# Sparse attention, dense FFN and soft MoE on one core: two transposes, four load places and one exponential moved

## The chip, the cores and the metric

The program runs on one core of one Trainium2 chip. The metric is the time of one execution on the device in microseconds (us). Several executions are timed and their median is given. One further execution is profiled, and all rows below come from that one. PE is the matrix engine, PEld its weight loads, DVE the vector engine, ACT the scalar engine, POOL GpSimd, SP the engine whose queue issues every DMA of this kernel.

## The reference

Three stages follow each other over 2304 tokens of 512 features, all in float32. The change lies in the third.

```python
x = attention(q, k, v)                 # 4 batches, 8 heads, 576 positions, local and strided masks
h = x @ w_in                           # 512 -> 2048
x = (h * sigmoid(1.702 * h)) @ w_out   # 2048 -> 512
logits = x @ phi                       # 512 -> 32 slots (8 experts of 4 slots)
d = exp(logits - logits.max(0)); d /= d.sum(0) + 1e-9       # softmax over the tokens
slot_input = d.T @ x                                        # 32 x 512
for e in range(8):                                          # experts, 512 -> 1024 -> 512
    slot_out[e] = relu(slot_input[e] @ w1[e]) @ w2[e]
c = exp(logits - logits.max(1)); c /= c.sum(1) + 1e-9       # softmax over the slots
out = c @ slot_out
```

## The kernel before

The tokens are worked through in five chunks, four of 512 and a last one of 256 (`CHUNKS`, numbers 0 to 4). For each chunk PE makes 16 blocks of `h` (line 489), ACT and DVE turn each into a gated block `gT` (lines 494 and 499), and DVE transposes it (line 527). The second matrix is never applied to the tokens: PE adds up logits from a product of `w_out` and `phi` (line 519), and `weighted` (line 626) adds up `u`, the gated blocks weighted by the slot softmax. Since the softmax over tokens needs the maximum of all tokens, each chunk lowers a running maximum (`nmx`), and the sums so far are scaled by `al`.

`combine_weights` makes the softmax over the slots of a chunk into `ca`. To be used on PE at the end, `ca` has to be split into a rounded part and the rest (`combine_split`, lines 639 and 640, tiles `c4`) and transposed on PE (`combine_t`, line 644, tiles `ctp`), and ACT copies the result to SBUF (`cT`, line 645).

`post_last` is the end of the last chunk. In order it does this: the last four logit products (line 656); the transposes of the combine weights of chunks 0 and 1; the logits repeated over the partitions (`lr`, line 667) and transposed (`lp`, line 674); the last maximum (DVE, lines 670 and 671); the exponential `l4` with its sum `zp` (ACT, line 679); its transposition `dT` (DVE, line 682); the sum `z` and its inverse, folded into `selz` (DVE, lines 684 to 690); `u` from `dT` (PE, line 626); the combine weights of chunk 4 (DVE and ACT, lines 710 to 718); and the copies of `u` out of PSUM (line 701). PE, DVE and ACT follow the written order here; POOL and SP don't. Then come `ut` (lines 699 and 882), its transposition (line 883), `spp` with `w_out` (line 890), `si`, the first expert products `hp` (`expand1`, line 922), the hidden transposes `hT` (line 933), the second expert products `op` (`expand2`, line 952) in three column groups of 256, 128 and 128, and after each group the final products `fp` (`combine`, line 968), whose copies leave by DMA (line 974). In the first column group, before the change, `expand2` number 5, 6 and 7 are each followed by the split and the transposes of one more chunk of combine weights (2, 3 and 4).

`load_ex` issues 36 loads of 1 MB: 0 to 3 are `w_out` (written earlier to DRAM), 4 to 19 the first expert matrices, 20 to 35 the second. Each load goes to the next free place: six in the pool `e1p` (tag `e`, loads 0 to 5), places of `x` tiles (tags `xA0`, `xA1`, `xB0`, `xB1`, `xC0`, `xC1`), places of `w_in` (tag `wi`) and quarters of `gT`. A load is issued when the last reader of its place is done, and the SP queue issues in order, so one load that waits holds up those behind it. Two tiles that are no loads also take `e` places: `hz`, the zero-padded hidden layer that POOL clears (line 980), and `hc`, the hidden layer before its transposition. A third, `fin`, holds the slot outputs.

Of the kernel before, what the change touches and what calls it, by code (L numbers as in the profile page):

```python
# [10 lines left out]
F32 = mybir.dt.float32  # L11
F32R = mybir.dt.float32r
# [5 lines left out]
AF = mybir.ActivationFunctionType  # L18
ALU = mybir.AluOpType
# [6 lines left out]
NS = NE * SPE  # L26
# [10 lines left out]
NF = FF // 128  # L37
# [43 lines left out]
def tile_kernel(ctx: ExitStack, tc: tile.TileContext, lqk, lv, sqk, sv, wraw, phi, wexp, cst, cstb, out):  # L81
    nc = tc.nc
# [53 lines left out]
    ca = keep.tile([P, NT // 128, NS], F32, name="ca")  # L136
    wp = keep.tile([P, NF, NS], F32, name="wp")
    
# [491 lines left out]

    def combine_split(c, parts):
        c0, N = CHUNKS[c]
        n = N // 128 // len(parts)
        c4s[c] = [t[:, 128 * k:128 * k + 128] for t in parts for k in range(n)]
        for k, t in enumerate(parts):
            c4 = t[:, :128 * n].rearrange("p (u r e q) -> p u r e q", r=2, e=2, q=8)
            ce = ca[:, c0 // 128 + n * k:c0 // 128 + n * k + n]
            cc = ce.rearrange("p t (j q) -> p (t j) q", q=8).unsqueeze(2).to_broadcast([P, 4 * n, 2, 8])
            nc.vector.tensor_copy(c4[:, :, :, 0].bitcast(F32R), cc)
            nc.vector.tensor_tensor(c4[:, :, :, 1].bitcast(F32R), cc, c4[:, :, :, 0], op=ALU.subtract)  # L640

# [5 lines left out]
    def post_last():  # L647
# [7 lines left out]
        def lg(j):  # L655
            nc.tensor.matmul(lgs[c][32 * j:32 * j + 32, :N], wp[:, NF - 4 + j, :], gs[c, NF - 4 + j][:, :N], start=False, stop=True)

        for j in range(3):
            lg(j)
# [17 lines left out]
        st["L"] = L  # L677
        zp = keep.tile([P, 1], F32, tag="zp", name=f"zp_{c}", bufs=2)
        nc.scalar.activation(l4[:, :N], lr[:, :N], AF.Exp, bias=nmx, accum_out=zp)
        al = keep.tile([P, 1], F32, tag="al", name=f"al_{c}", bufs=2)  # L680
        nc.scalar.activation(al, st["nm"], AF.Exp, scale=-1.0, bias=nmx)
        nc.vector.transpose(dT[:, :N], l4[:, :N])
        z = keep.tile([P, 1], F32, tag="z", name=f"z_{c}", bufs=2)
        nc.vector.scalar_tensor_tensor(z, st["z"], al, zp, op0=ALU.mult, op1=ALU.add)  # L684
        zi = keep.tile([P, 1], F32, name="zi")
# [179 lines left out]
    for s in side:  # L865
        for _ in s:
            pass
    load_ex(xp, "xB0")
    c = len(CHUNKS) - 1
    man = ctx.enter_context(ExitStack())  # L870
    man.enter_context(tc.manual_schedule(engines={mybir.EngineType.PE, mybir.EngineType.DVE, mybir.EngineType.Activation}))
    while todo:
        g_transpose(*todo.pop(0))
    ut, ub, halves, selz = post_last()
    for _ in range(2):
        load_ex(None, gx_tile())
# [20 lines left out]
    for h in range(2):  # L897
# [4 lines left out]
        st["si"] = (nc.vector.tensor_copy if h else nc.scalar.copy)(si[:, 2 * h:2 * h + 2], sip[:, :64].rearrange("p (k s) -> p k s", s=NS)).ins  # L902
    c4t = tl.tile([P, 2, 512], F32, name="c4t")
    cTs[3] = tl.tile([P, 512], F32R, name="cT3")
    moe_ps.close()
    ps_t = ctx.enter_context(tc.tile_pool(name="ps_t", bufs=3, space=PSUM))

    def ttile(name):
        return ps_t.tile([P, 512], F32, tag="t", name=name)

    hzt = e1p.tile([P, 2, 8, P], F32, tag="e", name="hz")
    hc = e1p.tile([P, 4, 512], F32, tag="e", name="hc")
    load_ex(e1p, "e")
    load_ex(xp, "xB1")
# [74 lines left out]
    expand1(1, 0)  # L989
    for _ in range(4):  # L990
        load_ex(wip, "wi")
    hidden_t(0, 1)
    expand1(1, 1)
    for _ in range(2):
        load_ex(wip, "wi")
    assert len(ex) == 36
# [3 lines left out]
    for n in range(8):  # L1000
        expand2(0, n)
        if n == 2:
            hidden_t(1, 1)
        if n >= 5:
            with tc.issue_after(st["si"]):
                combine_split(n - 3, [c4t[:, n % 2]])
            combine_t(n - 3, ttile(f"ctp_{n - 3}"))
    slot_out(0)
# [81 lines left out]
```

## Time and profile before

| | |
|---|---|
| median of 3 runs | 394.07 us (393.07 to 394.52) |
| profiled execution, its own time | 394.75 us |
| span of the profiled execution | 393.0 us |
| PE busy | 372.6 us, 95% of the span |
| DVE, ACT, POOL busy | 275.0, 214.5, 52.1 us |
| DMA | 91.25 MB, mean 232 GB/s |

The span runs from the first to the last instruction of the profiled execution; its own time lies 1.75 us above it. Busy shares are means over stages with different limits, so what the change touches has to be read from its own stretch, from 327 us to the end. PEclk in a row is the granted clock of PE as a share of the full 2.4 GHz: 0.50 is the lower of its two levels, 1.2 GHz.

### The profile page before, as it was taken

How to read it: one execution, taken by the hardware profiler on the slowest of the kernel's cores; microseconds unless marked ns; L12 is line 12 of the kernel's file. 1: busy time of each engine (PE TensorE's matmuls, PEld its weight loads, DVE VectorE, ACT ScalarE, POOL GpSimd, SP SyncE). 2: the span in 40 equal slices, each digit the busy share in tenths (PEclk: the TensorE clock that was granted, in tenths of full speed). 3: DMA queues.
4: the chain of work that ended last, by engine and by line, in shares of the span. 5: the costliest groups of instructions: out<-in, count | busy, mean ns of one | idle time of the engine just before them, and what ended most of it. 6: DMA issues, size and time to landing. Idle time of an engine off the chain costs nothing.

```text
span 393.0 us, 9638 instructions
## 1 busy us (share of the span) xinstructions
PE 372.6 (95%) x3874; PEld 261.2 (66%) x3875; DVE 275.0 (70%) x595; ACT 214.5 (55%) x585; POOL 52.1 (13%) x64
## 2 busy tenths in 40 slices
PE   8969999999999999999999899999999998899992
PEld 4757888877667574767476657767877786234682
DVE  3989899999788668988896888674446855321232
ACT  5977999899795745568446686302113123200331
POOL 1533346331020101001100010000000000100000
PEclk9988999999999999999999999999999999899997
DMA  8975294668753160497526646991008899879997
GB/s 300 416 293 200 81 327 143 228 211 311 262 199 111 53 207 9 129 319 267 203 86 196 200 150 214 315 398 78 0 2 318 332 330 362 304 282 419 420 373 237
DMA packets 29372, 91.25 MB, mean 232 GB/s; under 512 B 2448, under 2 KB 10768, under 8 KB 25232
## 3 DMA queue, kind: packets, MB, share of 16 engines
q1 hardware_dynamic: 29328, 90.64, 64.5%
q8 instruction: 30, 0.49, 0.5%
q14 instruction: 14, 0.11, 0.1%
HBM read 80.93 MB, written 8.91 MB: 229 GB/s over the span
## 4 chain that ended last, share of the span: by engine, by line
PE 64%; DVE 19%; ACT 10%; issue 2%; DMA 2%; POOL 0%; SPq 0%; ACTq 0%; DVEq 0%
PE h L489 38%; PE op L952 4%; ACT ts L273 4%; PE hp L922 4%; DVE gT L527 3%; PE av L333 2%; PE lg L519 2%; PE ptp L299 2%; PE u L626 2%; DMA raw<-wraw 2%; PE fp L968 2%; DVE nmx L260 2%; ACT neg L393 1%; PE s L219 1%; DVE acc L614 1%
## 5 line engine op out<-in xcount | busy, mean ns | idle before, releaser
L489 PE MATMUL h<-x,wi 128*128 128x512 f32 (+1 forms) x960 | 215.4, 377 | 0.5 <-DVE more L499 0.4
L489 PEld LDWEIGHTS h<-x,wi 128*128 128x128 f32 x960 | 165.4, 190 | 48.0 <-issue 14.6
L494 ACT ACTIVATE gT<-h 128x512 f32<-128x512 f32 (+1 forms) x50 | 27.0, 540 | 45.5 <-PE h L489 45.3
L284 POOL TENSOR_TENSOR ts<-ts,sm 128x384 f32<-128x384 f32 (+2 forms) x32 | 27.6, 862 | 140.0 <-DVE sm L280 112.5
L499 DVE SCALAR_TENSOR_TENSOR gT<-gT,h 128x512 f32<-128x512 f32 (+1 forms) x50 | 30.5, 612 | 21.2 <-ACT gT L494 20.9
L273 ACT ACTIVATE ts<-ts,nmx 128x96 f32<-128x96 f32 (+1 forms) x98 | 34.2, 352 | 9.1 <-DVE nmx L260 9.1
L393 ACT ACTIVATE neg<-raw,ebias 128x512 f32<-128x512 int16 x48 | 36.4, 759 | 0.0
L527 DVE STREAM_TRANSPOSE gT<-gT 128x512 f32<-128x512 f32 (+1 forms) x50 | 31.4, 633 | 2.0 <-PE lg L519 1.1
L428 POOL TENSOR_TENSOR wi<-wc,wi 128x512 fp32r<-128x512 f32 x16 | 21.7, 1369 | 31.8 <-ACT wi L424 31.8
L626 PE MATMUL u<-gT,dT 32*32 32x512 f32 x576 | 23.1, 633 | 2.4 <-DVE z L684 1.6
L494 ACT ACTIVATE more<-h 128x512 f32<-128x512 f32 (+1 forms) x19 | 10.6, 558 | 26.4 <-PE h L489 26.4
L299 PE MATMUL ptp<-cs,ts 128*96 128x128 f32 (+1 forms) x120 | 17.3, 278 | 6.0 <-POOL ts L284 3.4
L299 PEld LDWEIGHTS ptp<-cs,ts 128*96 128x96 f32 (+1 forms) x120 | 13.1, 132 | 11.2 <-POOL ts L284 6.0
L366 DVE TENSOR_TENSOR x<-av,x 128x320 fp32r<-128x320 f32 (+18 forms) x48 | 17.8, 403 | 1.2 <-ACT x L362 1.0
L362 ACT CAST x<-av 128x320 fp32r<-128x320 f32 (+18 forms) x48 | 16.2, 407 | 4.5 <-PE av L333 2.1
L273 ACT ACTIVATION_READ_ACCUMULATOR ts<-ts,nmx 128x1 f32 x98 | 18.6, 190 | 0.0
L626 PEld LDWEIGHTS u<-gT,dT 32*32 32x32 f32 x576 | 9.7, 104 | 12.4 <-issue 8.8
L519 PE MATMUL lg<-gT,wp 128*32 128x512 f32 (+1 forms) x92 | 17.7, 562 | 0.0
L333 PEld LDWEIGHTS av<-pt,v 96*64 96x64 f32 (+2 forms) x552 | 13.9, 136 | 4.6 <-issue 2.0
L499 DVE SCALAR_TENSOR_TENSOR more<-more,h 128x512 f32<-128x512 f32 (+1 forms) x19 | 12.0, 634 | 6.8 <-ACT more L494 6.4
L980 POOL MEMSET hz<- 128x512 f32 x4 | 1.9, 526 | 107.7 <-PE spp L890 107.7
L219 PE MATMUL s<-qk 64*64 64x96 f32 (+1 forms) x552 | 15.7, 236 | 0.3 <-DMA qk<-lqk 0.3
(173 smaller groups left out, 501.5 us busy)
## 6 DMA issues: line engine op xcount, KB each, us to landing
ex<-wexp SPq DMA_DIRECT2D x28, 1024.0 KB, 7.6
raw<-wraw SPq DMA_DIRECT2D x48, 511.8 KB, 4.4
v<-lv SPq DMA_DIRECT2D x8, 576.0 KB, 6.3
qk<-lqk SPq DMA_DIRECT2D x7, 608.0 KB, 6.8
wo_scr<-wo SPq DMA_DIRECT2D x16, 256.0 KB, 2.3
ex<-wo_scr SPq DMA_DIRECT2D x4, 1024.0 KB, 11.5
gT<-wexp SPq DMA_DIRECT2D x4, 1024.0 KB, 5.9
qk<-sqk SPq DMA_DIRECT2D x6, 604.0 KB, 5.7
```

Source lines behind the costliest of these rows:

```text
L273: nc.scalar.activation(ts[:, u], src[:, u], AF.Exp, scale=sc, bias=nmx[:, u:u + 1], accum_out=sm[:, u:u + 1])
L284: nc.gpsimd.tensor_tensor(ts, ts, sm[:, :nt].unsqueeze(2).to_broadcast([P, nt, nk]), op=ALU.mult)
L299: nc.tensor.transpose(ptp[:nk, u], src, ident)
L333: nc.tensor.matmul(avs[b, hp, e][64 * h:64 * h + 64, o:o + nq], v[k0:k0 + nk, P * w + 64 * h:P * w + 64 * h + 64], pt[k0:k0 + nk, p, 64 * ...
L393: nc.scalar.activation(n, top, AF.Relu, scale=-(2.0 ** 19), bias=ebias)
L428: nc.gpsimd.tensor_tensor(w[:, 1], conv.pop((f, 0)), w[:, 0].bitcast(F32), op=ALU.subtract)
L489: nc.tensor.matmul(h[:, :N], w[:, we, 128 * kt:128 * kt + 128], x[xe][:, kt, :N], start=kt + n == 0, stop=kt == 3 and n == 2)
L494: st["tanh"] = nc.scalar.activation(g[:, :N], hs[c, f][:, :N], AF.Tanh, scale=0.851).ins
L499: st["gate"] = nc.vector.scalar_tensor_tensor(g[:, :N], g[:, :N], 1.0, hs.pop((c, f))[:, :N], op0=ALU.add, op1=ALU.mult).ins
L519: nc.tensor.matmul(lgs[c][32 * j:32 * j + 32, :N], wp[:, f0 + j, :], gs[c, f0 + j][:, :N], start=f0 == 0, stop=f0 == NF - 4)
L527: nc.vector.transpose(t_slots(c)[:, f, :N], gs[c, f][:, :N])
L626: nc.tensor.matmul(us[a][32 * j:32 * j + 32, :].rearrange("p (t f) -> p t f", f=32), dT[q, 32 * b:32 * b + 32], gT[q, :, 32 * b:32 * b + 3 ...
```

## The change

The change has three parts.

First, the combine weights of chunks 2 and 3 are split and transposed in `post_last`. The split is done by POOL and ACT instead of DVE, into a new tile `c4x` at the place `xB0`, which the last chunk's `x` leaves free when the last product of `h` is done. The eight transposes stand on PE behind `lp`. ACT copies them behind `al`, chunk 3 to the place of `wp`. Because `c4x` now lies at `xB0`, load 21, which went there, is issued after `post_last`. The split and transposes of chunk 4 stay near the end, on DVE and PE.

Second, the last exponential is made in two halves of 128 columns, each with its own sum and its own transposition, and one addition joins the sums.

Third, two loads are asked for ahead of `hz` and `hc`, and two behind them, where it was one behind them. In the built program loads 24 to 27 now get the places of loads 0 to 3, `hz` that of load 5, `hc` that of load 4, and `fin` later that of `hc`. Before, load 24 got that of load 0, `hc` that of load 1, `hz` that of load 2, `fin` that of load 3. The loads behind move up by three places: the last, 35, takes the place of load 15 where it took that of load 18.

```diff
-    wp = keep.tile([P, NF, NS], F32, name="wp")
+    wp = keep.tile([P, NF, NS], F32, tag="wp", name="wp")
...
-    def combine_split(c, parts):
+    def combine_split(c, parts, high=nc.vector, low=nc.vector):
...
-            nc.vector.tensor_copy(c4[:, :, :, 0].bitcast(F32R), cc)
-            nc.vector.tensor_tensor(c4[:, :, :, 1].bitcast(F32R), cc, c4[:, :, :, 0], op=ALU.subtract)
+            (high.copy if high is nc.scalar else high.tensor_copy)(c4[:, :, :, 0].bitcast(F32R), cc)
+            low.tensor_tensor(c4[:, :, :, 1].bitcast(F32R), cc, c4[:, :, :, 0], op=ALU.subtract)
...
+        cx = xp.tile([P, 2, 512], F32, tag="xB0", name="c4x")
+        combine_split(3, [cx[:, 1]], nc.gpsimd, nc.gpsimd)
+        combine_split(2, [cx[:, 0]], nc.scalar, nc.gpsimd)
         for j in range(3):
             lg(j)
...
-        zp = keep.tile([P, 1], F32, tag="zp", name=f"zp_{c}", bufs=2)
-        nc.scalar.activation(l4[:, :N], lr[:, :N], AF.Exp, bias=nmx, accum_out=zp)
+        cTs[3] = keep.tile([P, 512], F32R, tag="wp", name="cT3")
+        ctps = [htile(f"ctp_{k}") for k in (2, 3)]
+        for k in (2, 3):
+            for n, t in enumerate(c4s[k]):
+                nc.tensor.transpose(ctps[k - 2][:, 128 * n:128 * n + 128], t, ident)
+        zp = keep.tile([P, 2], F32, name=f"zp_{c}")
+        for n in range(2):
+            t = slice(128 * n, 128 * n + 128)
+            nc.scalar.activation(l4[:, t], lr[:, t], AF.Exp, bias=nmx, accum_out=zp[:, n:n + 1])
+            nc.vector.transpose(dT[:, t], l4[:, t])
         al = keep.tile([P, 1], F32, tag="al", name=f"al_{c}", bufs=2)
         nc.scalar.activation(al, st["nm"], AF.Exp, scale=-1.0, bias=nmx)
-        nc.vector.transpose(dT[:, :N], l4[:, :N])
+        for k in (2, 3):
+            nc.scalar.copy(cTs[k], ctps[k - 2])
         z = keep.tile([P, 1], F32, tag="z", name=f"z_{c}", bufs=2)
-        nc.vector.scalar_tensor_tensor(z, st["z"], al, zp, op0=ALU.mult, op1=ALU.add)
+        nc.vector.scalar_tensor_tensor(z, st["z"], al, zp[:, 0:1], op0=ALU.mult, op1=ALU.add)
+        nc.vector.tensor_tensor(z, z, zp[:, 1:2], op=ALU.add)
...
-    load_ex(xp, "xB0")
...
     ut, ub, halves, selz = post_last()
+    load_ex(xp, "xB0")
...
+    for _ in range(2):
+        load_ex(e1p, "e")
     hzt = e1p.tile([P, 2, 8, P], F32, tag="e", name="hz")
     hc = e1p.tile([P, 4, 512], F32, tag="e", name="hc")
-    load_ex(e1p, "e")
+    for _ in range(2):
+        load_ex(e1p, "e")
     load_ex(xp, "xB1")
...
-        if n >= 5:
+        if n == 5:
             with tc.issue_after(st["si"]):
-                combine_split(n - 3, [c4t[:, n % 2]])
-            combine_t(n - 3, ttile(f"ctp_{n - 3}"))
+                combine_split(4, [c4t])
+        if n == 7:
+            combine_t(4, ttile("ctp_4"))
```

On PE, around the last maximum, the order was this (`lr` and `lp` are the two forms of the last logits, `ctp_3990` the transposes of chunk 1).

```order
-L665 MATMUL ctp_3990<-cs,gT 128x128 x4
-L667 MATMUL lr_3995<-l_4_3914,rep_r 128x256
-L674 MATMUL lp_4001<-rep_r,l_4_3914 128x32 x2
-L626 MATMUL u_0_4019<-gT,dT_3915 32x512 x4
-L626 MATMUL u_1_4020<-gT,dT_3915 32x512 x4
```

It is now this (`ctp_4010` and `ctp_4011` are the transposes of chunks 2 and 3).

```order
+L668 MATMUL ctp_3993<-cs,gT 128x128 x4
+L670 MATMUL lr_3998<-l_4_3914,rep_r 128x256
+L677 MATMUL lp_4004<-rep_r,l_4_3914 128x32 x2
+L685 MATMUL ctp_4010<-cs,c4x 128x128 x4
+L685 MATMUL ctp_4011<-cs,c4x 128x128 x4
+L626 MATMUL u_0_4038<-gT,dT_3915 32x512 x4
```

Eight transposes stand between `lp` and the first of `u`.

On PE, in the first column group of the second expert products, the order was this.

```order
-L952 MATMUL op_4265<-ex_4138,hz 32x256 x8
-L644 MATMUL ctp_4325<-cs,c4t 128x128 x4
-L952 MATMUL op_4265<-ex_4163,hz 32x256 x8
-L644 MATMUL ctp_4341<-cs,c4t 128x128 x4
-L952 MATMUL op_4265<-ex_4165,hz 32x256 x8
-L644 MATMUL ctp_4357<-cs,c4t 128x128 x2
```

It is now this (the same five products `op` from the fourth on).

```order
+L967 MATMUL op_4285<-gT,hz 32x256 x8
+L967 MATMUL op_4285<-ex_4154,hz 32x256 x8
+L967 MATMUL op_4285<-ex_4156,hz 32x256 x8
+L967 MATMUL op_4285<-ex_4160,hz 32x256 x8
+L967 MATMUL op_4285<-ex_4162,hz 32x256 x8
```

No transposes are left there; the two of chunk 4 moved ahead of the first hidden transposes.

On DVE, behind the last maximum, the order was this.

```order
-L671 TENSOR_TENSOR nmx_3998<-nmx_3998,nmx_3613 128x1
-L682 STREAM_TRANSPOSE dT_3915<-l_4_3914 128x256
-L684 SCALAR_TENSOR_TENSOR z_4011<-z_3623,al_4008,zp_4006 128x1
-L686 TENSOR_SCALAR zi<-z_4011 128x1
-L687 RECIPROCAL zi<-zi 128x1
```

It is now this.

```order
+L674 TENSOR_TENSOR nmx_4001<-nmx_4001,nmx_3613 128x1
+L690 STREAM_TRANSPOSE dT_3915<-l_4_3914 128x128 x2
+L696 SCALAR_TENSOR_TENSOR z_4029<-z_3623,al_4025,zp_4020 128x1
+L697 TENSOR_TENSOR z_4029<-z_4029,zp_4020 128x1
+L699 TENSOR_SCALAR zi<-z_4029 128x1
```

The transposition became two, and one addition stands ahead of the inverse; the rest of the DVE row, down to the copies of `u`, kept its order.

## Rows read from the trace of the kernel before

**Rows 1.** Chain that ended last, from 331 us on: start us, us, what.

```profile
332.75 3.53 PE u L626 x64
...
337.52 0.56 PE ut L882 x8
...
338.11 0.46 DVE dT L883
...
366.31 0.59 PE ctp L644 x4
...
386.10 0.37 ACT gT L971
```

**Rows 2.** Timeline, 327.8 to 333.2: start us, us, engine, line, operation [idle before].

```profile
327.93 0.38 ACT L494 ACTIVATE gT<-h 128x256 f32<-128x256 f32 x1 [1.05 <-PE h L489]
...
330.64 0.53 PE L674 MATMUL lp<-rep_r,l 128*128 128x32 f32 x4
...
331.56 0.47 ACT L679 ACTIVATE l<-lr,nmx 128x256 f32<-128x256 f32 x1
...
332.16 0.45 DVE L682 STREAM_TRANSPOSE dT<-l 128x256 f32<-128x256 f32 x1 [0.69 <-ACT l L679]
332.53 0.18 DVE L684 SCALAR_TENSOR_TENSOR z<-z,al,zp 128x1 f32<-128x1 f32 x1
```

**Rows 3.** PE alone in two stretches: busy (instructions), granted clock, DMA share, GB/s.

```profile
329.93:333.34 3.41, 1.83 (x41) 1.00 0.98 375
333.34:336.76 3.42, 3.42 (x71) 0.50 0.55 232
```

**Rows 4.** The products of line 626 alone, chunk 3: PE, PEld, clock, DMA.

```profile
303.00:308.00 5.00, 4.45 (x128) 2.20 (x128) 1.00 0.86 346
```

**Rows 5.** PE alone in two early stretches, columns as in rows 3.

```profile
15.90:19.32 3.42, 2.94 (x36) 1.00 1.03 419
19.32:22.73 3.41, 2.37 (x63) 1.00 1.04 415
```

**Rows 6.** Of these the transposes of line 299 alone: PE, PEld, clock, DMA.

```profile
15.90:19.32 3.42, 2.34 (x18) 1.84 (x18) 1.00 1.03 419
```

**Rows 7.** Timeline of DVE, 334.9 to 337.3.

```profile
335.00 0.22 DVE L718 TENSOR_TENSOR ca<-ca,cz 128x64 f32<-128x64 f32 x1
336.12 1.08 DVE L701 COPY gT<-u 128x256 f32<-128x256 f32 x3 [0.89 <-PE u L626]
```

**Rows 8.** POOL's instructions by line: shortest/median/longest in ns, first and last start.

```profile
L284 POOL TENSOR_TENSOR ts<-ts,sm x32: 720/830/1271, 12.5 to 233.6; 128x384 f32<-128x384 f32 x16, 128x480 f32<-128x480 f32 x8, 128x320 f32<-128x320 f32 x8
...
L428 POOL TENSOR_TENSOR wi<-wc,wi x16: 1265/1296/1759, 8.3 to 80.9; 128x512 fp32r<-128x512 f32 x16
```

**Rows 9.** DMA by stretch: length, granted clock, DMA share, GB/s.

```profile
334.00:350.00 16.00, 0.91 0.71 263
350.00:384.00 34.00, 1.00 1.02 405
...
386.00:390.00 4.00, 0.74 1.02 300
```

**Rows 10.** Last load, issued within 358.8 to 359.0: KB, us to landing.

```profile
ex<-wexp SPq DMA_DIRECT2D x1, 1024.0 KB, 20.2
```

**Rows 11.** Fifth output from the end: issue, and KB and us to landing.

```profile
385.23 0.77 SPq L974 DMA_DIRECT2D out<-gT  x1
...
out<-gT SPq DMA_DIRECT2D x1, 256.0 KB, 4.2
```

**Rows 12.** Last output: issue, and KB and us to landing.

```profile
388.83 0.82 SPq L974 DMA_DIRECT2D out<-gT  x1
...
out<-gT SPq DMA_DIRECT2D x1, 128.0 KB, 3.2
```

**Rows 13.** Small transfers elsewhere in the kernel, median us to landing.

```profile
wo_scr<-wo SPq DMA_DIRECT2D x16, 256.0 KB, 2.3
```

**Rows 14.** Timeline of PE, 381.7 to 383: the last second expert products.

```profile
381.78 1.08 PE L952 MATMUL op<-ex,hz 128*32 128x128 f32 x32
```

More of the change, by code (lines that the diff above doesn't have):

```diff
@@ L902, in tile_kernel @@
         st["si"] = (nc.vector.tensor_copy if h else nc.scalar.copy)(si[:, 2 * h:2 * h + 2], sip[:, :64].rearrange("p (k s) -> p k s", s=NS)).ins
-    c4t = tl.tile([P, 2, 512], F32, name="c4t")
-    cTs[3] = tl.tile([P, 512], F32R, name="cT3")
+    c4t = tl.tile([P, 256], F32, name="c4t")
     moe_ps.close()
@@ L989, in tile_kernel @@
     expand1(1, 0)
-    for _ in range(4):
-        load_ex(wip, "wi")
+    load_ex(wip, "wi")
     hidden_t(0, 1)
     expand1(1, 1)
-    for _ in range(2):
-        load_ex(wip, "wi")
     assert len(ex) == 36
```

## The prediction

> **What bounds the kernel now.** I read the page first. PE is busy 95% of the span, so a stretch counts only where PE waits or runs slowly, or where the end waits for something else. Then I read the chain that ended last, from 331 us on [rows 1]. It has two parts. Up to 338.11 it goes through the end of the last softmax: maximum, exponential, transposition, `u`, and the transposition of `ut`. From there it is PE nearly without a gap to the last products `fp`, and the last copy ends at 386.10 + 0.37 = 386.47.
>
> In the timeline [rows 2] the reader should see PE's only long gap here: `lp` ends at 331.17, `u` begins at 332.75 [rows 1]. PE has nothing to do in the 1.58 us in which ACT makes the exponential and DVE transposes it. The windows on PE [rows 3] show the price of that gap. PE is busy 1.83 of 3.41 us from 329.93 on, and from 333.34 to 336.76 its granted clock is 0.50, the lower level. `u` falls into it: 64 products in 3.53 us [rows 1], 0.055 us each, where chunk 3 did 128 in 4.45 us at the full clock [rows 4], 0.035 each. At that rate 64 take 2.23 us, so the fallen clock costs `u` alone 1.30 us.
>
> The DMA windows [rows 9] show a second bound. From 334 to 350 the transfers are busy 0.71 of the time, so 16 x 0.29 = 4.6 us lie idle while loads wait for places. From 350 to 384 they are at 1.02 without a break, and in 386 to 390 again, when only outputs are left. The fifth output from the end lands 4.2 us after its issue [rows 11], the last one 3.2 us [rows 12], at 388.83 + 3.2 = 392.0; elsewhere in the kernel as small a transfer lands in 2.3 us [rows 13]. So the outputs queue behind something, and part of the last 5 us is DMA, not PE.
>
> **Part 1a, transposes beside the last maximum.** Eight transposes move. In the tail each group of four takes 0.59 us on the chain [rows 1], and there are two such groups: 2 x 0.59 = 1.18 us leave PE's path. In their new place they run from 331.17 to 332.35, inside the gap, if their input is ready. The input comes from POOL: one copy and two subtractions of 128x256 each, after the last product of `h`, that is from about 327.93, when ACT's activation of it begins [rows 2]. POOL shows no copy and no such form. The nearest rows are 128x320 to 128x480 at 0.72 to 1.27 us and 128x512 at up to 1.76 us [rows 8]. Three at the shortest, 0.72, give 2.2 us and readiness at 330.1; three at the longest, 1.76, give 5.3 us and 333.2. By size these are smaller than any of them, so I take 2.2 us: 1 us ahead of need. If that cover went, each us beyond 3.2 would push `u` by one. ACT's own copy of chunk 2 stands behind the activation at 327.93 and ahead of the copy of chunk 0's transposes, for which ACT waits anyway; its two copies to `cT` follow `al`, in the time in which DVE is at `z` and its inverse and asks nothing of ACT. I cost them at nothing; if that cover were gone they would hold up line 713 and with it line 718.
>
> **Part 1b, the clock.** With the transposes PE is busy nearly without a gap to the start of `u`, so I expect the clock to stay at 1.00 and `u` to take 2.23 us. Does transposing hold the clock? From 15.90 to 19.32 PE is busy 2.94 us [rows 5], 2.34 of them transposes [rows 6], and the clock stays at 1.00 in that stretch and the next. By this row it holds. The Trainium skill ("TensorE: Matmul & The Clock Gate", Part 4: PE-mode transpose) says otherwise, that the full clock does not engage for transposes because they don't count as PE work in the same way. By that rule the clock would fall here as before; the early stretch speaks against it. The rule is priced as a rival below.
>
> **Part 2, the halved exponential.** The whole one runs from 331.56, and its transposition starts 0.60 us later and takes 0.45 [rows 2]. A half has 128 columns less; from these rows I estimate its transposition to start near 332.0 and take 0.3, so that `u` starts near 332.4, 0.3 us sooner. The second half ends near 332.3, its transposition near 332.6, and `u` needs it 1.1 us after its start. But DVE's row goes on: `z` at 332.53 [rows 2] stays about there, and the added joining of the sums puts 0.2 us (0.18 for line 684, [rows 2]) ahead of everything up to line 718.
>
> **What is late next.** With `u` ending at 332.4 + 2.23 = 334.65, its copies no longer wait for PE but for DVE, which finishes line 718 at 335.22 now [rows 7] and 335.42 then. Two copies of 0.36 (1.08 for three, [rows 7]) end at 336.14, the last products of `ut` need about 0.5 more (0.56 for eight, [rows 1]), so the transposition at line 883 starts near 336.7 instead of 338.11 [rows 1]: 1.4 us sooner. The 0.3 us of the halved exponential is thereby hidden; it counts only where the clock stays low. Bounds: 0.3 us if it does, 1.5 if the half works out a little better.
>
> **Part 3, the loads.** Loads 24 to 27 are issued as `spp` reads loads 0 to 3, where one of them could go before. Load 21 moves back from the last product of `h` to about 332.4, gated by the transposes, and holds up the two `gT` loads behind it not at all, since these wait for `u`. The idle 4.6 us of DMA are largely filled. PE gains nothing by it: the last load now lands at 358.9 + 20.2 = 379.1 [rows 10] and its product starts after 381.78 [rows 14]. That cover of 2.7 us would be used up by the 2.6 us that PE gains, so without the earlier loads the gain would be at its limit; with them it has room. `hz` waits for load 5 and `hc` for load 4, both read early in the first expert products, well before DVE writes into `hz`. The outputs gain: the loads end sooner by up to the 4.6 us filled and by what PE gains, so that outputs don't queue behind them. The last five hold 1.15 MB, 3.9 us at 300 GB/s [rows 9]. Their first issue moves from 385.23 to 382.6; landing after 2.3 [rows 13] instead of 4.2 us and then one per 0.88, the last lands near 388.1, instead of 392.0. That is 3.9 in all, 1.3 beyond PE's 2.6. The lower bound is zero, if the queue stays as long. I take 0.8.
>
> **The sum.** 1.4 + 1.18 + 0.8 = 3.4 us. Against the profiled execution, 394.75, that gives 391.35. The median is 0.7 below it and the fastest run, 393.07, 1.7 below, about what a fall of the clock costs, so some executions may not have it. For such a one only 1.18 + 0.8 less 0.2 for the addition is to gain: 393.07 - 1.8 = 391.3. Both meet, and I say **391.3**.
>
> **Rivals.** *The clock falls anyway*, by the transposes not holding it or by the short gaps that now lie near 335.6 and 336.8. For it: in rows 3 a busy time of 1.83 of 3.41 was followed by the low level, and the new gaps lie close together. Against it: rows 5 and 6. Then 0.3 + 1.18 + 0.8 = 2.3 remain: 392.5. The page's rule gives just this case. Chance 0.16. *The loads are not what holds the outputs*, as their landing is simply slow: 1.4 + 1.18 = 2.6, so 392.1. For it: DMA is also full in 386 to 390 with outputs alone. Chance 0.11. *POOL is late*, the slower side: at 5.3 us `u` starts at 333.2 + 1.2 = 334.4, 1.7 later than now, the clock falls as before, 1.18 is won in the tail, and 0.5 is lost: 395.2. It turns to a loss where the three take over 4.8 us. Against it: every POOL row of less than 480 columns. Chance 0.05. *More*: outputs take the whole 1.3 and an execution starts from the median: near 390.2. Chance 0.05. The forecast, 390.4 to 392.0 as its own range, keeps 0.63.
>
> **How the numbers follow.** A measurement of this kernel tells about 0.5% from no change, that is below 392.1 for faster and above 396.0 for slower. Faster: the forecast, the larger gain, and some of the first two rivals, 0.71. Within: the rest of these and most of the late POOL, 0.26. Slower: 0.03. The range is 390.0 to 393.5; it takes in both clocks and both prices of the outputs and leaves the late POOL out.
>
> **What would show it.** In the changed profile: the eight transposes between 331 and 332.5, PEclk 1.00 from 330 to 340, `u` in 2.2 to 2.3 us, the first copy of `u` waiting for DVE and not PE, line 883's transposition near 336.7; no `ctp` but one pair in the tail; DMA share near 1 from 335 to 370 and the last load landed by 372; the last outputs landing in less than 3.5 us. The prediction is wrong if POOL's three take over 3.2 us, if the clock has a stretch at 0.50 behind 330, or if the last output still lands 5.5 us behind the last copy.

## The result, and the profile after

| | before | after |
|---|---|---|
| median of 8 runs each, us | 394.45 (393.07 to 396.25) | 391.25 (389.44 to 392.48) |
| ratio, 95% interval | | 0.9918 (0.9895 to 0.9941) |
| profiled execution: own time, span | 394.75, 393.0 | 391.47, 389.7 |

Faster by 0.8%. To see where, I cut both spans at the same four events: the start of the last maximum (DVE), the start of the first transposition of `ut` (line 883, now 896), the end of the last copy, the end of the span.

| us | before | after | gain |
|---|---|---|---|
| to the start of the last maximum | 330.85 | 331.63 | -0.78 |
| from there to the transposition of `ut` | 7.26 | 6.10 | 1.16 |
| from there to the end of the last copy | 48.36 | 46.56 | 1.80 |
| from there to the end of the span | 6.53 | 5.41 | 1.12 |

The last three rows are what the change touches: 4.08 us. The first lies ahead of it. There, in the window from 23 to 26 us, the granted clock is 0.59 in this execution and 1.00 in the one of before; the experiments below show this start anywhere from 330.28 to 332.50 in kernels with the same instructions up to there. These starts go with the length of an early stretch at 0.50, which begins between 23 and 27 us: where it lasts about 10 us (after, and five kernels of the experiments), the last maximum starts at 331.63 to 332.50, where it lasts about 7 us (before, and four others) at 330.28 to 331.30. Both lengths occur with the change and without it.

Chain of waits after, from the last exponential on: start, us, what.

```profile
333.18 0.31 DVE dT L690
...
336.08 0.23 DVE ca L731
...
336.31 0.35 DVE gT L714
...
336.70 1.01 PE ut L895 x8
...
337.73 0.46 DVE dT L896
...
350.99 0.37 PE ctp L644 x2
351.36 0.44 PE hT L948 x4
...
363.43 6.20 PE op L967 x144
```

In [rows 1] the first part of the chain ran through PE's `u`. Now it runs through DVE, with one step on ACT (line 726), from 333.18 to the copies of `u`: DVE is what is late. Further down, `op` is one run of 144 (6.20 us); before, it was cut three times by transposes. The same chain before, beside the lines of [rows 1]:

```profile
363.59 2.73 PE op L952 x48
...
366.90 1.00 PE op L952 x16
...
368.49 1.00 PE op L952 x16
369.49 0.37 PE ctp L644 x2
369.86 1.88 PE op L952 x64
```

Timeline after, POOL and PE around the last maximum, and DVE's copies.

```profile
328.80 0.40 POOL L639 CAST c4x<-ca 128x256 fp32r<-128x256 f32 x1 [93.77 <-PE h L489]
329.28 1.43 POOL L640 TENSOR_TENSOR c4x<-ca,c4x 128x256 fp32r<-128x256 f32 x2
...
331.79 1.07 PE L685 MATMUL ctp<-cs,c4x 128*128 128x128 f32 x8
333.20 2.35 PE L626 MATMUL u<-gT,dT 32*32 32x512 f32 x64 [0.34 <-DVE dT L690]
...
336.23 1.08 DVE L714 COPY gT<-u 128x256 f32<-128x256 f32 x3
```

POOL is done at 330.71, 1.1 us before PE begins the transposes. PE waits 0.34 us for `u` where it waited 1.58, and `u` takes 2.35 instead of 3.53 [rows 1].

Windows of PE after, the stretches of [rows 3]: the granted clock (third figure from the right) stays at 1.00.

```profile
329.93:333.34 3.41, 3.07 (x36) 1.00 0.83 315
333.34:336.76 3.42, 3.27 (x82) 1.00 0.83 271
```

DMA windows after, as [rows 9], then the last load and the last output (issue; KB and us to landing).

```profile
334.00:350.00 16.00, 1.00 0.97 396
350.00:384.00 34.00, 1.00 0.99 381
```

```profile
355.43 0.33 SPq L749 DMA_DIRECT2D ex<-wexp  x1
...
ex<-wexp SPq DMA_DIRECT2D x1, 1024.0 KB, 18.9
...
385.56 0.83 SPq L989 DMA_DIRECT2D out<-gT  x1
...
out<-gT SPq DMA_DIRECT2D x1, 128.0 KB, 3.2
```

The idle DMA time of [rows 9] is gone (0.97 for 0.71). The last load lands at 374.3, before at 379.1 [rows 10]. The last output is issued 1.3 us behind the last copy (385.56 less 384.29), before 2.4 us [rows 12], and lands after the same 3.2 us.

### The profile page after: what moved, and what is told of

The parts are those of the page before. It is cut to its first block, busy times and chain, and to the rows that moved or that the text cites. A ratio compares the mean times of both kernels' runs of the same rounds, so it can differ in the third digit from the quotient of the medians.

```text
span 389.7 us, 9640 instructions
## 1 busy us (share of the span) xinstructions
PE 372.4 (96%) x3875; PEld 262.1 (67%) x3875; DVE 274.2 (70%) x593; ACT 215.0 (55%) x588; POOL 53.9 (14%) x67
## 4 chain that ended last, share of the span: by engine, by line
PE 58%; DVE 25%; ACT 10%; issue 3%; DMA 2%; POOL 0%; SPq 0%; ACTq 0%; DVEq 0%; POOLq 0%
PE h L489 34%; ACT ts L273 4%; PE op L967 4%; PE hp L937 4%; DVE gT L527 3%; PE lg L519 2%; PE ptp L299 2%; PE av L333 2%; DVE nmx L260 2%; DMA raw<-wraw 2%; PE fp L983 2%; DVE x L366 1%; DVE gT L499 1%; DVE wc L397 1%; ACT neg L393 1%
## 5 line engine op out<-in xcount | busy, mean ns | idle before, releaser
L299 PE MATMUL ptp<-cs,ts 128*96 128x128 f32 (+1 forms) x120 | 18.2, 288 | 5.7 <-POOL ts L284 3.3
L626 PE MATMUL u<-gT,dT 32*32 32x512 f32 x576 | 22.0, 597 | 1.1 <-DVE dT L590 0.4
L333 PE MATMUL av<-pt,v 96*64 96x64 f32 (+2 forms) x552 | 15.8, 224 | 0.1
```

The costliest lines, as they stand in the source:

```text
L299: nc.tensor.transpose(ptp[:nk, u], src, ident)
L333: nc.tensor.matmul(avs[b, hp, e][64 * h:64 * h + 64, o:o + nq], v[k0:k0 + nk, P * w + 64 * h:P * w + 64 * h + 64], pt[k0:k0 + nk, p, 64 * ...
L626: nc.tensor.matmul(us[a][32 * j:32 * j + 32, :].rearrange("p (t f) -> p t f", f=32), dT[q, 32 * b:32 * b + 32], gT[q, :, 32 * b:32 * b + 3 ...
```

## The experiments

One table for all. "Max" is the start of the last maximum; the next three columns are the stretches of the table above; "sum" is from the maximum to the end of the span. The ratio is to runs of the kernel before on the same chip. The medians come from several chips, so two of them are compared by their ratios: the kernel before gave 395.10 where the four runs from "loads alone" to "whole exponential" were timed, 394.40 with the fills and the late weights, 394.86 with "POOL late" and "traffic early", 394.26 with "traffic late" and 393.65 with "chunk 3 alone". The columns between are from one profiled execution each.

| kernel | max | to `ut` | to last copy | to end | sum | median | ratio (95%) |
|---|---|---|---|---|---|---|---|
| before | 330.85 | 7.26 | 48.36 | 6.53 | 62.15 | 394.45 | |
| after | 331.63 | 6.10 | 46.56 | 5.41 | 58.07 | 391.25 | 0.9918 (0.9895 to 0.9941) |
| loads alone | 331.98 | 7.27 | 48.62 | 5.23 | 61.12 | 394.21 | 0.9984 (0.9963 to 1.0006) |
| transposes alone | 331.70 | 5.81 | 47.56 | 7.23 | 60.60 | 394.34 | 0.9972 (0.9953 to 0.9991) |
| after, old loads | 330.28 | 6.11 | 47.55 | 7.16 | 60.82 | 394.74 | 0.9993 (0.9969 to 1.0017) |
| after, whole exponential | 332.50 | 5.81 | 46.52 | 5.57 | 57.90 | 390.96 | 0.9901 (0.9873 to 0.9930) |
| before, products as fill | 330.87 | 5.81 | 48.37 | 6.15 | 60.33 | 394.39 | 0.9983 (0.9960 to 1.0006) |
| before, transposes as fill | 331.99 | 5.80 | 48.38 | 6.43 | 60.61 | 393.84 | 0.9983 (0.9960 to 1.0006) |
| after, POOL late | 334.01 | 6.52 | 46.53 | 5.24 | 58.29 | 393.65 | 0.9972 (0.9950 to 0.9995) |
| after, POOL late, chunk 3 alone | 330.15 | 6.38 | 46.55 | 5.22 | 58.15 | 391.72 | 0.9935 (0.9909 to 0.9962) |
| after, traffic early | 331.30 | 6.10 | 46.55 | 5.45 | 58.10 | 391.36 | 0.9905 (0.9879 to 0.9931) |
| after, traffic late | 330.95 | 6.11 | 51.67 | 7.47 | 65.25 | 396.58 | 1.0051 (1.0025 to 1.0078) |
| after, weights late | 332.19 | 5.49 | 46.53 | 5.29 | 57.31 | 390.09 | 0.9889 (0.9859 to 0.9919) |
| weights late and early fill | 329.38 | 5.50 | 46.55 | 6.37 | 58.42 | 388.76 | 0.9851 (0.9817 to 0.9884) |

**Loads alone.**

```diff
+    for _ in range(2):
+        load_ex(e1p, "e")
     hzt = e1p.tile([P, 2, 8, P], F32, tag="e", name="hz")
     hc = e1p.tile([P, 4, 512], F32, tag="e", name="hc")
-    load_ex(e1p, "e")
+    for _ in range(2):
+        load_ex(e1p, "e")
```

> The kernel before with the third part of the change alone: two loads are asked for ahead of hz and hc and two behind them. My account: PE's row does not change. u stays near 3.5 us after a stretch at the lower clock, the transposition at line 883 stays about 6.8 us behind the last maximum, and the last copy of the program stays where it was measured from that maximum, within 0.3 us. The loads end some 3 us sooner, and the last output lands nearer to the last copy: the span behind the last copy, 6.5 us in the kernel before (393.0 less 386.47), falls to about 5.4, so the profile gains 0.8 to 1.1 us and the time goes from 394.4 to about 393.4. Rival, the loads are not what holds the outputs: 6.5 us stay behind the last copy and the time is 394.4. Rival, the loads also hold PE in the expert products: then PE's last copy moves too, by more than 0.5 us.

The outputs gain 1.30 (6.53 to 5.23), and the last copy stays within 0.3 us of its place: both as expected. That the time falls is not shown: the ratio's interval takes in 1. The 48.62 hides two changes. The tail of the program is not in written order, and with other loads the scheduler also put the transposes of chunks 2 to 4 ahead of the first hidden ones. Chain of waits there:

```profile
352.51 0.60 PE ctp L644 x4
...
353.13 0.46 ACT cT L645
...
354.09 0.62 ACT hc L930
...
354.76 0.66 PE hT L936 x4
```

ACT copies two `cT` before it makes `hc`, so the hidden transposes start 2.25 us behind the 64 first expert products ahead of them (352.51 to 354.76). PE fills 1.45 us of that with the moved transposes and idles 0.80. The second expert products gain most of it back, since no transposes cut them any more.

**Transposes alone, and the changed kernel with the old loads.** The first also has the exponential whole.

```diff
-    for _ in range(2):
-        load_ex(e1p, "e")
     hzt = e1p.tile([P, 2, 8, P], F32, tag="e", name="hz")
     hc = e1p.tile([P, 4, 512], F32, tag="e", name="hc")
-    for _ in range(2):
-        load_ex(e1p, "e")
+    load_ex(e1p, "e")
...
```

The loads that are not asked for here come later, in places of `w_in`, as in the kernel before.

> The changed kernel with the old order of the loads around hz and hc and with the exponential whole, so that mainly the moved transposes are left (load 21 still goes out behind the last chunk). My account: the clock has no stretch at 0.50 behind 330 us, u takes 2.3 to 2.4 us, the transposition at line 883 comes 1.1 to 1.3 us sooner behind the last maximum than before, and the part of PE from there to the last copy is 1.8 us shorter. So PE's last copy is 2.9 to 3.0 us sooner behind the maximum; the outputs still wait behind the loads, and the time falls from 394.4 to about 391.9 (2.5 us). Rival, without the earlier loads PE reaches the second expert products before their data: then part of PE's gain, up to 1 us, is lost in waits of op for ex, and the time is about 393. Rival, the halved exponential is needed for the gain: u ends 0.3 us later and so does line 883.

> The changed kernel with the old order of the loads around hz and hc. My account: PE's row and its last copy stand where they stand in the changed kernel, within 0.3 us behind the last maximum; what follows the last copy grows from 5.4 us (389.7 less 384.29) to 6.2 or more, so the time goes from 391.25 to about 392.2. Rival, the loads do not matter: 391.25. Rival, the loads have become the bound of the expert products since PE is sooner there: op waits for ex, and the time is 393 or more.

Up to `ut` PE gains what was expected or a little more (1.45 us against 1.1 to 1.3). But the times, 394.34 and 394.74, miss the 391.9 and 392.2 that were expected: behind `ut` two things go against it. What follows the last copy grows to 7.2 us, as long as the loads are issued late: without part 3 a faster PE only makes its outputs wait longer. DMA windows with the old loads:

```profile
334.00:350.00 16.00, 1.00 0.83 317
```

And the tail gains 0.8 instead of 1.8. That I had not expected: with the old loads the scheduler leaves the transposes of chunk 4 inside `op` (chain of waits there: `op` on both sides of this line), and moves four of the final products from behind the last `op` to ahead of it.

```profile
366.32 0.37 PE ctp L644 x2
```

No `op` waits for its load in either kernel; that rival falls.

First with the old loads, then after, PE at the last `op` (start, us; idle before it in brackets):

```profile
379.25 1.08 PE L964 MATMUL op<-ex,hz 128*32 128x128 f32 x32
381.20 2.00 PE L980 MATMUL fp<-fin,cT 128*128 128x128 f32 x16 [0.87 <-DVE fin L970]
```

```profile
379.59 1.08 PE L967 MATMUL op<-ex,hz 128*32 128x128 f32 x32
380.60 0.44 PE L983 MATMUL fp<-fin,cT 128*128 128x128 f32 x2
380.88 0.38 PE L983 MATMUL fp<-fin 128*128 128x128 f32 x2
381.55 2.00 PE L983 MATMUL fp<-fin,cT 128*128 128x128 f32 x16 [0.28 <-DVE fin L973]
```

After, four products fill the wait for `fin` (0.28 idle); with the old loads PE idles 0.87. So taking part 3 back costs 2.75 us of the sum (60.82 less 58.07): 1.75 in the outputs, 1.0 in the order that PE gets. The last is an effect of the scheduler, not of the transfers.

**Whole exponential.**

```diff
-        for n in range(2):
-            t = slice(128 * n, 128 * n + 128)
-            nc.scalar.activation(l4[:, t], lr[:, t], AF.Exp, bias=nmx, accum_out=zp[:, n:n + 1])
-            nc.vector.transpose(dT[:, t], l4[:, t])
+        nc.scalar.activation(l4[:, :N], lr[:, :N], AF.Exp, bias=nmx, accum_out=zp[:, 0:1])
+        nc.vector.transpose(dT[:, :N], l4[:, :N])
...
-        nc.vector.tensor_tensor(z, z, zp[:, 1:2], op=ALU.add)
```

> The changed kernel with the last exponential whole again, with one transposition, and without the addition that joins the sums. My account: the half is hidden, because DVE and not PE sets the copies of u. u starts some 0.3 us later behind the last maximum, DVE's line 731 ends 0.1 to 0.3 us sooner, since the addition is gone, and the transposition at line 896 stands within 0.2 us of its place behind the maximum; the time is 391.25 or 0.1 to 0.2 less. Rival, the half counts in full: line 896 comes 0.3 us later and the time is 391.55. Rival, the wait of PE in front of u becomes long enough for the clock to fall: a stretch at 0.50 behind 330 us, u at 3.5 us, and the time is 392.3.

```profile
336.66 0.22 DVE L728 TENSOR_TENSOR ca<-ca,cz 128x64 f32<-128x64 f32 x1
...
338.31 0.45 DVE L893 STREAM_TRANSPOSE dT<-ut 128x256 f32<-128x256 f32 x1 [0.43 <-PE ut L892]
```

In this timeline of DVE the last of the weights starts 4.16 us behind the maximum (336.66 less 332.50), after the change 4.45 (336.08 less 331.63), and `ut` is transposed 0.29 sooner. Part 2 is not hidden at nothing: it costs 0.3 us in the profile, since DVE is the late engine and got one more transposition and one more addition. The same 0.30 lies between "transposes alone" (5.81), where the exponential is whole, and the changed kernel with the old loads (6.11). The ratios, 0.9901 and 0.9918, can't tell these apart.

**Fills.** The kernel before, with work on PE that nothing needs, in the gap ahead of `u`.

```diff
+        ft = htile("fill")
+        for _ in range(3):
+            nc.tensor.matmul(ft[:, :N], rep, acc[:, 0, :N], start=True, stop=True)
```

> The kernel before with three more products of 128x256 on PE between lp and u, whose result nothing reads. They take about 1.0 us of PE's gap of 1.6 us and do none of the change's work. My account: the clock has no stretch at 0.50 behind 330 us; u takes 2.3 to 2.4 us instead of 3.53 and starts where it did (1.9 us behind the start of the last maximum); DVE is then late and not PE, so that the transposition at line 883 starts 1.2 to 1.5 us sooner behind the maximum, at 5.8 to 6.1 us instead of 7.26. Of that the outputs give some back, since they wait behind the loads: 0.5 to 1.0 us off the time are left. Rival, the clock falls by itself at this place whatever PE does: u stays at 3.5 us and line 883 at 7.2.

```diff
+        for k in range(2):
+            ft = htile(f"fill_{k}")
+            for n in range(4):
+                nc.tensor.transpose(ft[:, 128 * n:128 * n + 128], acc[:, k, 128 * n:128 * n + 128], ident)
```

> The kernel before with eight more transposes of 128x128 on PE between lp and u, whose result nothing reads: the same instructions that the change puts there, about 1.07 us, without its work. My account: transposes hold the clock as products do, no stretch at 0.50 behind 330 us, u takes 2.3 to 2.4 us, and the transposition at line 883 starts 5.8 to 6.1 us behind the last maximum, as with three products. Rival, transposes do not hold the clock, and in the changed kernel it was held by something else: u stays near 3.5 us after a stretch at 0.50, and line 883 near 7.2 us. The Trainium skill (TensorE: Matmul & The Clock Gate, Part 4: PE-mode transpose) says that transposes do not count as PE work in the same way, and by that rule the rival holds.

PE's timeline and windows with the eight transposes:

```profile
332.15 1.07 PE L678 MATMUL fill<-cs,acc 128*128 128x128 f32 x8
333.80 2.35 PE L626 MATMUL u<-gT,dT 32*32 32x512 f32 x64 [0.58 <-DVE dT L686]
```

```profile
331.00:333.80 2.80, 2.22 (x18) 1.00 0.96 372
333.80:336.20 2.40, 2.40 (x68) 1.00 0.91 375
```

Both fills give `u` in 2.35 us at a clock of 1.00 and `ut` 1.45 us sooner. So the gap is what lets the clock fall, and transposes close it as well as products do. All profiles agree: a stretch at 0.50 within 10 us behind the start of the last maximum stands only in the three kernels where PE sat idle 1.57 us (loads alone), 1.58 (before) or 2.00 (POOL late) before `u`; in the other eleven no idle time of PE there is longer than 1.07 us.

The sum falls by 1.8 and 1.5 us, the time by less than can be told: single runs go from 392.7 to 395.0, and before on that chip from 392.6 to 396.7. The fills thus take away the slow end and leave the fast one. That would fit executions of the kernel before in which the clock doesn't fall, which the prediction supposed; with one profiled execution of each kernel it is not shown.

**POOL late.**

```diff
         cx = xp.tile([P, 2, 512], F32, tag="xB0", name="c4x")
+        for _ in range(3):
+            nc.gpsimd.memset(cx, 0.0)
```

> The changed kernel with POOL made late on purpose: three clears of c4x (128x1024, whose contents are then overwritten) stand on POOL ahead of the split of chunks 2 and 3. Each is estimated at about 1.05 us from POOL's clears of hz (1.92 us for four of half that size), so the split ends some 2.1 to 3.2 us later, at 1.2 to 2.2 us behind the start of the last maximum, where it ended 0.9 us ahead of it in the changed kernel. My account of the rival that the prediction priced: PE's eight transposes wait for POOL, u starts 2.3 to 3.4 us behind the start of the maximum instead of 1.57, DVE's lateness hides 0.7 us of that, and the transposition at line 896 comes 6.5 to 7.2 us behind the maximum with the clock at 1.00, or up to 8.4 with a stretch at 0.50, since PE now has a gap of 1.5 us or more. The last copy moves by as much: the time is 0.4 to 2.3 us above the changed kernel's 391.25. Rival, the transposes are not on the path to u: line 896 stays at 6.1.

The second kernel clears `cx[:, 1]` alone, five times.

> The changed kernel with POOL made late again, but by five clears of the half of c4x that belongs to chunk 3 alone (128x512, then overwritten), so that ACT's copy for chunk 2 no longer waits for POOL. In the run with clears of the whole tile that copy waited, and with it the copy of the last logits behind it on ACT, so that the whole end of the softmax came 2.5 us late. Five clears at half of its 0.97 us are 2.4 us: the split ends 1.5 us behind the start of the last maximum instead of 0.9 ahead of it. My account: the maximum itself is not late; PE's transposes end near 2.6 us behind it, u starts 1.0 to 1.2 us later than in the changed kernel (2.6 to 2.8 us behind the maximum), and DVE's lateness hides most of that if the clock stays at 1.00: the transposition at line 896 then comes 6.3 to 6.7 us behind the maximum instead of 6.10. If PE's gap lets the clock fall as in the kernel before, u takes 3.3 to 3.5 us and line 896 comes 7.4 to 7.9 us behind it. The time is 391.5 to 393. Rival, ACT or DVE is held up all the same: the maximum itself comes later than POOL's clears explain.

The first did not do what I meant: ACT's copy for chunk 2 waited for the clears, and the copy of the last logits stands behind it on ACT, so `lr` and the maximum came late, not the transposes. PE's timeline and windows:

```profile
333.27 0.70 PE L672 MATMUL lr<-l,rep_r 128*128 128x256 f32 x2 [2.00 <-ACT l L667]
...
335.59 3.36 PE L626 MATMUL u<-gT,dT 32*32 32x512 f32 x64
```

```profile
330.00:333.00 3.00, 1.27 (x8) 1.00 1.00 358
...
335.00:338.20 3.20, 3.20 (x53) 0.52 0.49 120
```

After a wait of 2.0 us the clock falls again, and `u` takes 3.36. The second does what the rival needs:

```profile
332.02 0.66 PE L687 MATMUL ctp<-cs,c4x 128*128 128x128 f32 x4 [1.07 <-POOL c4x L640]
...
332.60 2.35 PE L626 MATMUL u<-gT,dT 32*32 32x512 f32 x64
```

`u` starts 2.45 us behind the maximum instead of 1.57; `ut` comes 0.28 later. DVE's lateness hides 0.6 of the 0.88, and through PE's wait of 1.07 us the clock stayed at 1.00.

**Traffic.** 2 MB that nobody reads.

```diff
+    dup = scr.tile([2, P, 4 * DM], F32, name="dup")
...
+    for k in range(2):
+        nc.sync.dma_start(dup[k], wexp[k])
     load_ex(xp, "xB1")
```

> The changed kernel with two more transfers of 1 MB (from the expert matrices to an unused place in DRAM) behind the loads that the third part brings forward; PE, DVE and ACT keep every instruction and its order. My account: from 340 on DMA has no idle time left in the changed kernel (share 1.02), so 2 MB more, about 5 us at 420 GB/s and perhaps twice that since they are written to DRAM as well, come out at the end: first the outputs land later (5.4 us behind the last copy in the changed kernel, 8 us or more here), and if the second expert loads come late too, op waits for ex and PE's last copy moves as well. The time is 3 to 8 us longer. Rival, the loads are not what holds the outputs, which land slowly by themselves: under 1 us.

This tested nothing of the end. The transfers waited for nothing and were issued at 27.6 and 40.7 us; there 2 MB cost nothing that can be told (sum 58.10 for 58.07, ratio 0.9905 for 0.9918). So they were taken from `acc_s`:

```diff
+        nc.sync.dma_start(dup[k], acc_s.unsqueeze(1).to_broadcast([P, 4, DM]))
```

> The changed kernel with 2 MB of transfers that nothing reads, written from acc_s to an unused place in DRAM; since acc_s is ready at about 343 us, they cannot run earlier, and they stand in SP's queue ahead of the last eight loads. On PE the order of some products in the last two column groups differs, which was worth 0.7 us in other runs. My account: from 340 to 375 DMA has no idle time in the changed kernel, so 2 MB more (5 us at 420 GB/s) come out at the end. The last loads land up to 5 us later, the last second expert products wait for them by 1 to 3 us, and the outputs stand behind the loads: from the start of the last maximum to the end of the span it takes 61 to 64 us instead of 58.07, and the time is 394 to 397. Rival, the outputs land slowly by themselves and the loads have slack: under 1 us more.

Chain of waits at its end:

```profile
343.34 17.50 DMA dup<-acc_s
...
360.91 21.31 DMA ex<-wexp
...
382.27 1.12 PE op L970 x32
...
384.22 4.12 PE fp L986 x18
```

7.2 us more in the sum: the last `op` waits for the last load (382.22), `fp` behind it runs at the lower clock (4.12 for 2.35), and the span ends 7.47 us behind the last copy. Measured from the maximum, the last load lands 8.6 us later than in the changed kernel (51.3 for 42.7) and the last `op` starts 3.3 later (51.3 for 48.0): for PE the last load of the changed kernel had 5.3 us to spare.

For the outputs there is less. In each of the fourteen profiles, take how long the last load has landed when the last copy ends. Where it is 9.0 to 11.8 us (seven kernels, the changed one among them with 10.0), the span ends 5.2 to 5.6 us behind the last copy; at 7.4 to 7.8 us (before, both fills, late weights with early fill) 6.1 to 6.5; at 6.5 to 6.8 us (both kernels with the old loads, traffic late) 7.2 to 7.5. So the loads hold the outputs where they land less than 8 to 9 us ahead of the last copy; beyond that, earlier loads gain nothing, and 5.2 us stay.

**Weights late**, and that with the early gap filled.

```diff
-        combine_weights(c)
...
         st["si"] = (nc.vector.tensor_copy if h else nc.scalar.copy)(si[:, 2 * h:2 * h + 2], sip[:, :64].rearrange("p (k s) -> p k s", s=NS)).ins
+    combine_weights(c)
```

> The changed kernel with the combine weights of chunk 4 (lines 723 to 731) made behind the copies of si instead of ahead of the copies of u. My account: in the changed kernel these seven DVE instructions, and the wait for ACT among them, take from 334.64 to 336.31 and hold up the copies of u, which PE has ready at 335.55. Without them the copies start when u ends, 0.7 us sooner, and the transposition at line 896 starts 5.3 to 5.5 us behind the last maximum instead of 6.10. The weights have time: their transposes stand 14 us later. So 0.6 to 0.8 us come off PE's last copy, and 0.4 to 0.7 off the time, 390.6 to 390.9. Rival, PE is late as well, and its ut for the running part ends where DVE's copies end now: then under 0.2 us. Rival, the later weights hold up the copies that the first hidden transposes wait for: then up to 0.5 us is lost there.

```profile
335.94 1.09 DVE L713 COPY gT<-u 128x256 f32<-128x256 f32 x3 [0.65 <-PE u L626]
...
337.68 0.45 DVE L895 STREAM_TRANSPOSE dT<-ut 128x256 f32<-128x256 f32 x1 [0.65 <-PE ut L894]
```

Now DVE waits for PE ahead of the copies, and `ut` comes 0.61 sooner. The ratio, 0.9889, is not told from the 0.9918 of the changed kernel. PE is the late engine here, with the exponential on its chain, so the halves should count in this kernel; it was not run with the whole one.

```diff
-... N.0.3.1 T.0.2.0 P.0.3.0 B W.1.0 ...
+... N.0.3.1 B B B T.0.2.0 P.0.3.0 B B B B B B W.1.0 ...
-... C.0.2.1D T.0.3.0 R.5 ...
+... C.0.2.1D B B B T.0.3.0 R.5 ...
```

> The kernel of the run above (combine weights of chunk 4 late) with nine more of the dummy products that the kernel already uses, in the early stretch from 20 to 26 us where PE waits for the attention of the first batch, so that PE idles less there. My account: in the changed kernel the clock is at 0.50 from 23.5 to 33.75, in the kernel before from 26.14 to 32.97, and the start of the last maximum differs by up to 2.2 us between the profiles so far (330.28 to 332.50), which is this stretch. With the gap filled the stretch is shorter or gone: the last maximum starts 1 us or more ahead of 331.6, the times spread less, and the median is 0.5 to 1.5 us below that of the run above, 389.3 to 390.2. Rival, PE is not what the early stretch waits for (it is ACT and the loads), and the clock there costs nothing: no difference. Rival, the dummy products stand ahead of work that is ready and cost their own time, nine times 0.2 us: up to 1.9 us slower.

The fill is eleven products, not the nine of the expectation. Windows of PE in the early stretch, first without, then with it:

```profile
23.00:26.00 3.00, 1.25 (x5) 0.57 1.00 395
26.00:30.00 4.00, 4.00 (x95) 0.50 0.44 130
```

```profile
23.00:26.00 3.00, 2.62 (x16) 1.00 1.00 399
26.00:30.00 4.00, 4.00 (x100) 1.00 0.50 150
```

The early stretch at 0.50 is gone and the maximum starts at 329.38. The median is 1.3 us below the run without the fill on the same chip, and the ratio, 0.9851, lies clear of the changed kernel's 0.9918: the fastest version. The runs do not spread less (387.45 to 389.75; without the fill 389.48 to 391.24), which was expected. Of what the start gains, 1.1 us goes back into the outputs (6.37 for 5.29): the last load lands only 0.9 us sooner (373.9 for 374.8), the last copy 2.8.

## Why the prediction was right, and where its terms were off

**The time.** 391.3 was said, 391.25 measured. The agreement is closer than the terms, and that is luck: 1.16 + 1.80 + 1.12 = 4.08 us were gained where the sum had 3.4, and in this execution the last maximum came 0.78 later, with its longer early stretch at 0.50. None of the three signs of being wrong came: POOL took 1.9 us, the clock stayed at 1.00 from the maximum to the last copy, and the last output landed 4.5 us behind the last copy.

**Part 1a, POOL's split.** Taken as 2.2 us, from 327.93 to 330.1; it took 1.9 and left 1.1 us of cover, where 1 was said. The late-POOL run shows that 0.6 us of a delay of `u` would have been hidden besides, so the rival of the late POOL was priced too high.

**Part 1b, the clock.** Right: both fills isolate it; `u` took 2.35 us for the 2.23 that were said. The run with the transposes decides the question that the prediction weighed: with nothing added but eight transposes the clock stayed at 1.00. The Trainium skill (TensorE: Matmul & The Clock Gate, Part 4: PE-mode transpose) says that transposes don't count as PE work in the same way; by that rule the clock would have fallen here too, and no run here agrees with it. These are fp32 transposes that the profile lists as MATMUL with the identity; whether they are the mode that the page means, no row tells.

**What is late next: 1.4 us said, 1.16 measured.** The mechanism, DVE late and not PE, was right. The 0.25 us that are missing stand in two places. DVE finished the weights (line 731) 4.68 us behind the start of the maximum, where the sum has 4.57: the halved exponential, charged with the 0.2 of one addition, costs 0.3 on just that chain. The two copies that the first transposition of `ut` needs took 0.67 us for the 0.72 that were said (they end at 336.98; the third is for the second half of `ut`), but from their end to the transposition it took 0.75 where 0.56 was counted. With the exponential whole the term would have been 1.45.

**The tail: 1.18 said, 1.80 measured.** Two groups of four transposes are 2 x 0.59. Left out were: chunk 4's two, which also leave `op` (0.37) and cost 0.22 in their new place (0.37 + 0.44 for `ctp` and `hT` after, 0.59 for `hT` alone elsewhere); and the restarts of `op`: 48 + 16 + 16 + 64 took 2.73 + 1.00 + 1.00 + 1.88 = 6.61 us before, 144 in one run 6.20, that is 0.41. Together 1.18 + 0.37 - 0.22 + 0.41 = 1.74. The remaining 0.06 is spread over the final products. The order listing showed chunk 4's move; it was named there and not priced.

**Part 3, the outputs: 0.8 said, 1.12 measured.** Right in kind, and the rival that the loads don't hold the outputs falls with the loads alone and with the late traffic; the 5.2 us that stay behind early loads they don't explain. What shrank is the time to the issue of the last output (2.4 to 1.3 us behind the last copy). The landing in 2.3 us of [rows 13], from which the term was built, was not reached: the fifth output from the end took 2.7 us (4.2 before), the last one 3.2 as before. And I priced the part from the state before. Against a PE already faster it is worth 1.75 in the outputs and 1.0 in PE's order, where the prediction had PE gain nothing by it; the 1.0 is the scheduler's and not a wait for a load. Part 1 without part 3 keeps 1.55 us of the sum and 0.3% of the time. The loads were to have landed by 372; the last landed at 374.3.

**Open:** the medians differ by 3.2 us, the profiles by 4.08 from the maximum on. The start ahead of the maximum varies by more than the difference. It goes with the early stretch at 0.50, of which both lengths occur with the change and without it; how often each occurs, one profiled execution of a kernel can't tell.

## What to carry to other kernels

When two resources end together (here PE and the queue of loads and outputs), cost each part of a change against the kernel that has the other parts, not against the old one: alone, part 3 gained 0.2% (not told from nothing) and part 1 0.3%, together 0.8%. About 1 us of the difference is here an order of PE's work that came with the loads, so compare the orders on the engines too when only transfers are moved. Before splitting an operation to feed one engine sooner, look which engine is late behind it: the split added its overhead to that one. And a rule about the clock is checked cheaply by putting just the disputed instructions into the gap, with results that nobody reads.

## What the runs showed of the hardware that was not expected

- 2 MB of transfers cost nothing that can be told at 27 to 41 us (from the expert matrices) and 7.2 us from 343 on (from `acc_s`).
- A late load costs twice: PE waits for it, and what follows runs at the lower clock (18 `fp` in 4.12 us, 2.35 elsewhere).
- Ahead of `u`, the clock fell to 0.50 behind idle times of PE of 1.57, 1.58 and 2.00 us and stayed at 1.00 behind one of 1.07; eight fp32 transposes of 128x128 in the gap kept it at 1.00 like three products of 128x256.
- Eleven dummy products, put around a stretch where PE was busy 1.25 of 3.00 us, kept the clock at 1.00 there, and the maximum some 300 us later started at 329.38, in one profiled execution; the undisturbed kernels without them start it at 330.15 to 332.50.
